# Attention keys and values on 128 partitions instead of 96, in a kernel of linear attention and two GELU-like layers

## The chip, the cores and the metric

The kernel runs on one core of a Trainium2 chip. The metric is device time in microseconds (us), the median of several executions. Engines that matter: TensorE (PE), with its weight loads (PEld), VectorE (DVE), ScalarE (ACT), GpSimd (POOL), and SyncE (SP), which here only issues DMAs.

## The reference

Shapes: q, k and v are 4 batches x 8 heads x 576 tokens x 64, all float32; x has 2304 tokens of 512 features; both layers go 512 to 2048 and back.

```
q_s = softmax(q, over the 64 features of a token)
k_s = exp(k - max over the 576 tokens) / (sum over the 576 tokens + 1e-9)   # per feature
kv  = einsum('bhsd,bhse->bhde', k_s, v)          # 64 x 64 for each head
att = einsum('bhsd,bhde->bhse', q_s, kv)
x   = att with heads side by side                # 2304 x 512
x   = layer(x, w_in1, w_out1, g(h) = h * sigmoid(1.702 h))
out = layer(x, w_in2, w_out2, g(h) = h * tanh(softplus(h)))
```

## The kernel before

Every large matmul is written as three fp32r matmuls on a high and a low part of each operand, and DVE and ACT split activations and weights into these parts. Tokens go in six blocks of 384. For a block the attention makes `xt`; the first layer makes `h` (line 755), the gate (lines 768 and 773) and `acc` (line 796). When all six blocks are through the first layer, the second follows (lines 755 into `hp`, 929 into `acc`). The weights arrive as raw words and are decoded by ACT and DVE (`weight`, lines 380 to 409) while the first block is computed.

The order of all work is written out by `Plan`: each operation is entered with its engines, an estimated cost, and what it reads and writes, and a list scheduler with six forward and backward passes picks the order and, where there are two ways, the engine. Engines then run their lists in order. SP issues all DMAs, one after the other (line 320, in `dma`).

Keys and values are handled by units: one unit is a pair of heads of one batch, so there are 16, four for each batch. Blocks 0, 1, 3 and 4 start a batch (`fresh`), and so make four units each; blocks 1 and 4 hold tokens of two batches. A unit does this:

- `k_load` and `v_load`: one DMA puts 576 tokens of both heads on 96 partitions, six tokens in each, in `kt`. In the first batch v lands packed in `vr` and ACT copies it (line 450) into `vt`, whose rows have two more columns of ones; later v goes straight into `vt`, one DMA for each head, in pieces of 256 bytes.
- `k_max`: three DVE maxima (line 476) bring six tokens of a partition to one, PE transposes the 96 x 128 result (line 481) and DVE takes the maximum along the row (line 482).
- In batches 0 and 1 `k_first`: for each head PE adds k and minus the maximum in PSUM by two matmuls of 384 columns (lines 494 and 497), and ACT takes exp from there (line 510). In batches 2 and 3 `k_later`: PE spreads the maximum (line 520), DVE subtracts (line 522), ACT takes exp (line 523).
- `k_kv`: for each head six matmuls (line 533) contract 96 tokens each and accumulate 64 x 66 values; the head picks the half of the output partitions. Then come a reciprocal and a scaled copy (lines 545 to 565).

In the trace each float32 matmul stands as two records of two passes; a transpose stands as one.

Of the kernel before, what the change touches and what calls it, by code (L numbers as in the profile page):

```python
# [8 lines left out]
F32 = mybir.dt.float32  # L9
# [201 lines left out]
def tile_attention_moe_moe(  # L211
# [21 lines left out]

    nc = tc.nc
    P = 128
# [9 lines left out]
    KC = 6  # L245
    KP = S // KC
# [3 lines left out]
    ND = 3  # L250
    SPLIT = ((0, 0), (0, 1), (1, 0))
# [26 lines left out]
    kt = [ap.tile([KP, 2, KC, D], F32, name=f"kt{i}") for i in range(2)]  # L278
    vt = [ap.tile([KP, 2, KC, D + 2], F32, name="vt0")]
    qt = ap.tile([P, NCT, 4, D], F32, name="qt")  # L280
    kv = [ap.tile([P, 2, P], F32R, name=f"kv{i}") for i in range(NHP)]
    pmt = [ap.tile([KP, P], F32, name=f"pmt{i}") for i in range(NHP)]
# [3 lines left out]
    kx = [ap.tile([KP, 2, 3, D], F32, name=f"kx{i}") for i in range(2)]  # L286
    rs = ap.tile([P, NHP], F32, name="rs")
    qs = ap.tile([P, 2, 12], F32, name="qs")

# [3 lines left out]
    kt += [sp.tile([KP, 2, KC, D], F32, name=f"kt{i}") for i in range(2, NHP)]  # L293
    vt += [sp.tile([KP, 2, KC, D + 2], F32, name=f"vt{i}") for i in range(1, NHP)]
    vr = [sp.tile([KP, 2, KC * D], F32, name=f"vr{i}") for i in range(2)] + [gt2[0:KP]]
# [5 lines left out]
    for t in vt:  # L301
        nc.gpsimd.memset(t[:, :, :, D : D + 2], 1.0)
# [15 lines left out]
    def dma(size, reads, writes, out, in_, slow=1):  # L318
        plan.op(
            [(DMA, max(size * slow / 280.0, 650.0), lambda: nc.sync.dma_start(out=out(), in_=in_()), False)],  # L320
            reads,
            writes,
        )
# [93 lines left out]
    def k_tile(u):  # L417
        return u if u < NHP else u % 2

    def v_tile(u):  # L420
        return u if u < NHP else 0

    def k_load(u):
        b, hp = divmod(u, NHP)
        dma(
            S * 512,
            [],
            [("kt", k_tile(u))],
            lambda: kt[k_tile(u)],
            lambda: k[b, 2 * hp : 2 * hp + 2].rearrange("h (p c) d -> p h c d", c=KC),  # L430
        )

    def v_load(u):
        b, hp = divmod(u, NHP)
        key = ("vt", v_tile(u))
        if b == 0:

            dense, dk = vr[hp % 3], [("vr", hp % 3)] if hp % 3 < 2 else [("gt", 0), ("gt", 1)]
            dma(
                S * 512,  # L440
                [],
                dk,
                lambda: dense,
                lambda: v[b, 2 * hp : 2 * hp + 2].rearrange("h (p c) d -> p h (c d)", c=KC),
            )
            to = vt[v_tile(u)][:, :, :, 0:D]
            of = dense.rearrange("p j (c d) -> p j c d", d=D)
            plan.op(
                [
                    (ACT, act_ns(768), lambda: nc.scalar.activation(out=to, in_=of, func=AF.Copy), False),  # L450
                    (POOL, 1200.0, lambda: nc.gpsimd.tensor_copy(out=to, in_=of), True),
                ],
                dk,
                [key + (j,) for j in range(2)],
            )
            return
        for j in range(2):
            dma(
                S * 256,
                [],  # L460
                [key + (j,)],
                lambda j=j: vt[v_tile(u)][:, j, :, 0:D],
                lambda j=j: v[b, 2 * hp + j].rearrange("(p c) d -> p c d", c=KC),
                slow=2,
            )

    def k_max(u, ps, key):

        kk = ("kt", k_tile(u))
# [4 lines left out]
        xk = ("kx", u % 2)  # L474
        largest = lambda n, out, in0, in1, reads, writes: dve(
            n, reads, writes, lambda: nc.vector.tensor_tensor(out=out, in0=in0, in1=in1, op=ALU.max), pair=True
        )
# [4 lines left out]
        dve(96, [key], [mk], lambda: nc.vector.reduce_max(out=m, in_=ps, axis=AX.X))  # L482

    def k_first(u, ps, keys):


        kk, mk = ("kt", k_tile(u)), ("mc", u % NHP)
        t, m = kt[k_tile(u)], mcol[:, u % NHP : u % NHP + 1]
        k_max(u, ps[0][:, NB : NB + KP], keys[0])
        for j in range(2):  # L490

            def less(j=j):
                o = ps[j][0:KP, 0:NB]
                nc.tensor.matmul(
                    out=o, lhsT=ident[0:KP, 0:KP], rhs=t[:, j].rearrange("p c d -> p (c d)"), start=True, stop=False
                )
                nc.tensor.matmul(
                    out=o.rearrange("p (c d) -> p c d", d=D),
                    lhsT=m.to_broadcast([P, KP]),
                    rhs=minus[:, j * D : (j + 1) * D].rearrange("p (o d) -> p o d", o=1).to_broadcast([P, KC, D]),  # L500
                    start=False,
                    stop=True,
                )

            pe(1330, [("kt", k_tile(u)), ("kt", k_tile(u), j), mk], [keys[j]], less, whole=True)
            act(
                NB,
                [keys[j]],
                [("kt", k_tile(u), j)],
                lambda j=j: nc.scalar.activation(  # L510
                    out=t[:, j].rearrange("p c d -> p (c d)"), in_=ps[j][0:KP, 0:NB], func=AF.Exp
                ),
                psum=True,
            )

    def k_later(u, ps1, ps2, key):
        kk, mk = ("kt", k_tile(u)), ("mc", u % NHP)
        t, m = kt[k_tile(u)], mcol[:, u % NHP : u % NHP + 1]
        k_max(u, ps1[:, 0:KP], key)
        pe(110, [mk], [key], lambda: nc.tensor.transpose(ps2[0:KP, :], m.to_broadcast([P, KP]), ident))  # L520
        far = ps2[0:KP, :].rearrange("p (j o d) -> p j o d", j=2, o=1).to_broadcast([KP, 2, KC, D])
        dve(768, [kk, key], [kk], lambda: nc.vector.tensor_tensor(out=t, in0=t, in1=far, op=ALU.subtract))
        act(768, [kk], [kk], lambda: nc.scalar.activation(out=t, in_=t, func=AF.Exp))

    def k_kv(u, ps3, key3):
        kk = ("kt", k_tile(u))
        t = kt[k_tile(u)]

        def mm():
            w = vt[v_tile(u)]  # L530
            for j in range(2):
                for c in range(KC):
# [8 lines left out]
        pe(1375, [kk] + [("kt", k_tile(u), j) for j in range(2)] + [("vt", v_tile(u), j) for j in range(2)], [key3], mm, whole=True)  # L541
# [51 lines left out]
    def q_soft(blk, half):  # L593
# [18 lines left out]
        either(768, ALU.subtract, flat, flat, wide, key + [sk], key)  # L612
        act(768, key, key, lambda: nc.scalar.activation(out=flat(), in_=flat(), func=AF.Exp))
        dve(768, key, [sk], lambda: nc.vector.reduce_sum(out=s, in_=flat(), axis=AX.X))
        dve(12, [sk], [sk], lambda: nc.vector.tensor_scalar_add(s, s, 1e-9))
# [347 lines left out]
    def idle():  # L963
# [9 lines left out]
        + [("kt", i) for i in range(2, NHP)]  # L973
        + [("vt", i, j) for i in range(1, NHP) for j in range(2)]
        + [("vr", i) for i in range(2)]
        + [("qr", i) for i in range(2)],
# [9 lines left out]
    for n in range(NS):  # L986
# [14 lines left out]
        if n == NS - NFC:  # L1001
            plan.op(
                [(NONE, 0.0, pool_second, False)],
                [],
                [("second",)]
                + [("kt", i) for i in range(2)]
                + [("vt", 0, j) for j in range(2)]
                + [("qt", j, d) for j in range(4) for d in (0, 192)]
                + [("kv", hp, a, j) for hp in range(NHP) for a in range(2) for j in range(2)]
                + [("kv32", hp, j) for hp in range(NHP) for j in range(2)]  # L1010
                + [(s, i) for s in ("qT32", "kx") for i in range(2)]
                + [("pm", i) for i in range(NHP)]
                + [(s, i) for s in ("mc", "rs") for i in range(NHP)]
                + [("qs", i) for i in range(2)],
            )
# [54 lines left out]
```

## Time and profile before

| | us |
|---|---|
| median of 3 runs | 892.26 (891.75 to 892.71) |
| the profiled execution, its own time | 892.4 |
| its span, first to last instruction | 890.6 |
| PE busy in the span | 880.1 |
| DVE busy | 395.7 |
| ACT busy | 361.6 |

A group's mean duration is that of one instruction from its start to its end, and neighbours overlap; so the price of a matmul in a stream is the distance between starts. Slices and windows tell where an engine is full; only there does its time set the pace.

### The profile page before, as it was taken

The page shows a single profiled execution, that of the slowest core. Times are in us where ns is not written, and L with a number is a line of the kernel's source. Part 1 is how long each engine was busy: PE and PEld are TensorE (multiplying, and loading weights), DVE is VectorE, ACT ScalarE, POOL GpSimd, SP SyncE. Part 2 cuts the span into 40 slices and gives each one's busy share as a digit, 9 for nine tenths or more (in the row PEclk, how much of TensorE's full clock was granted, in tenths as well). Part 3 has the DMA queues.
Part 4 walks back from the last instruction along what each step waited for, and adds up shares of the span by engine and source line. Part 5 has one row for each costly group of instructions (what it writes and reads, how often), then busy time and mean ns, then how long its engine had stood idle before and what let it go on. Part 6 is the DMA issues. An engine that isn't in the chain of part 4 may idle for free.

```text
span 890.6 us, 12257 instructions
## 1 busy us (share of the span) xinstructions
PE 880.1 (99%) x4961; PEld 819.4 (92%) x4961; DVE 395.7 (44%) x760; ACT 361.6 (41%) x649; POOL 5.3 (1%) x21
## 2 busy tenths in 40 slices
PE   8999999999999999999999999999999999999998
PEld 5797899999999999999999999899899899899897
DVE  7999993263385276226999911101101101101101
ACT  5987873242353244224778821311321321321321
POOL 1000000000000000000000000000000000000000
PEclk9999999999999999999999999999999999999999
DMA  9676762011132021100355302001001001000001
GB/s 249 202 224 181 202 208 72 1 36 71 27 90 99 1 71 45 59 1 18 118 167 187 120 1 71 36 1 71 36 1 71 36 1 71 36 1 0 36 1 36
DMA packets 63145, 65.80 MB, mean 74 GB/s; under 512 B 32497, under 2 KB 54513, under 8 KB 62577
## 3 DMA queue, kind: packets, MB, share of 16 engines
q1 hardware_dynamic: 63088, 65.02, 24.2%
q8 instruction: 39, 0.64, 0.3%
q14 instruction: 18, 0.14, 0.0%
HBM read 54.00 MB, written 11.01 MB: 73 GB/s over the span
## 4 chain that ended last, share of the span: by engine, by line
PE 90%; DVE 5%; ACT 2%; DMA 2%; issue 1%; SPq 0%; DVEq 0%
PE hp L755 23%; PE acc L929 22%; PE acc L796 20%; PE h L755 20%; PE at L533 1%; DVE dec L393 1%; DVE dec L398 1%; DMA raw<-in_moe_w_in_dram 1%; PE at L667 1%; PE at L638 1%; DVE W L329 1%; PE at L676 1%; DMA raw<-in_moe_w_out_dram 1%; DVE gt L773 1%; DVE g L329 0%
## 5 line engine op out<-in xcount | busy, mean ns | idle before, releaser
L755 PE MATMUL h<-xt,W 128*128 128x384 f32 x1152 | 224.0, 339 | 1.0 <-DVE gt L773 0.8
L796 PE MATMUL acc<-g,W 128*128 128x384 f32 x1152 | 223.2, 339 | 0.1
L755 PE MATMUL hp<-xt,W 128*128 128x384 f32 x1152 | 208.4, 336 | 0.0
L929 PE MATMUL acc<-W,g 128*128 128x512 f32 x864 | 206.1, 392 | 0.0
L755 PEld LDWEIGHTS hp<-xt,W 128*128 128x128 f32 x1152 | 201.9, 188 | 3.7
L755 PEld LDWEIGHTS h<-xt,W 128*128 128x128 f32 x1152 | 200.7, 188 | 4.4 <-DVE gt L773 1.1
L796 PEld LDWEIGHTS acc<-g,W 128*128 128x128 f32 x1152 | 200.6, 188 | 2.8 <-issue 0.8
L929 PEld LDWEIGHTS acc<-W,g 128*128 128x128 f32 x864 | 161.7, 188 | 32.6
L329 DVE TENSOR_TENSOR g<-gt,g 128x384 fp32r<-128x384 f32 (+1 forms) x110 | 67.4, 613 | 178.8 <-ACT g L337 178.5
L329 DVE TENSOR_TENSOR g<-tb,g 128x768 fp32r<-128x768 f32 x32 | 30.6, 958 | 211.5 <-ACT g L337 211.5
L904 ACT ACTIVATE tb<-hp 128x768 f32<-128x768 f32 x32 | 26.0, 813 | 177.6 <-PE hp L755 177.6
L337 ACT ACTIVATE g<-gt 128x384 fp32r<-128x384 f32 (+1 forms) x112 | 63.7, 569 | 80.1 <-PE acc L796 78.0
L768 ACT ACTIVATE gt<-h 128x384 f32<-128x384 f32 x96 | 46.8, 487 | 92.2 <-PE h L755 91.9
L773 DVE SCALAR_TENSOR_TENSOR gt<-gt,h 128x384 f32<-128x384 f32 x96 | 52.7, 549 | 63.5 <-ACT gt L768 63.3
L904 ACT ACTIVATE gt<-hp 128x768 f32<-128x768 f32 x16 | 13.0, 813 | 96.3 <-PE hp L755 96.3
L346 ACT ACTIVATE dec<-raw 128x512 f32<-128x512 f32 x64 | 42.9, 675 | 11.0 <-DVE W L329 8.2
L346 ACT ACTIVATE raw<-raw 128x512 int32<-128x512 uint32 x63 | 42.1, 677 | 6.1 <-DMA raw<-in_moe_w_out_dram 4.5
L329 DVE TENSOR_TENSOR W<-dec,W 128x512 fp32r<-128x512 f32 x64 | 43.6, 684 | 0.7 <-ACT W L337 0.5
L398 DVE CUSTOM_DVE_ANT_0 dec<-raw,dec 128x1024 uint16<-128x1024 uint16 x64 | 43.6, 683 | 0.4
L393 DVE SCALAR_TENSOR_TENSOR dec<-raw,dec 128x512 int32<-128x512 int32 x64 | 43.6, 683 | 0.2
L337 ACT ACTIVATE W<-dec 128x512 fp32r<-128x512 f32 x62 | 38.7, 628 | 5.8 <-DVE dec L398 5.8
L337 ACT ACTIVATE g<-tb 128x768 fp32r<-128x768 f32 x32 | 27.1, 846 | 1.0
(79 smaller groups left out, 397.0 us busy)
## 6 DMA issues: line engine op xcount, KB each, us to landing
raw<-in_moe_w_in_dram SPq DMA_DIRECT2D x32, 512.0 KB, 4.2
raw<-in_moe_w_out_dram SPq DMA_DIRECT2D x32, 512.0 KB, 4.0
x2d<-xt SPq DMA_DIRECT2D x16, 384.0 KB, 3.1
xt<-x2d SPq DMA_DIRECT2D x4, 1536.0 KB, 6.5
kt<-in_k_dram SPq DMA_DIRECT2D x16, 288.0 KB, 4.5
out_dram<-dec SPq DMA_DIRECT2D x15, 256.0 KB, 2.1
vt<-in_v_dram SPq DMA_DIRECT2D x24, 144.0 KB, 3.2
qt<-in_q_dram SPq DMA_DIRECT2D x24, 96.0 KB, 2.7
```

The lines of the kernel that those rows point to most:

```text
L329: return lambda: engine.tensor_tensor(out=out(), in0=in0(), in1=in1(), op=op)
L337: (ACT, act_ns(n), lambda: nc.scalar.activation(out=out(), in_=in_(), func=AF.Copy), False),
L346: (ACT, act_ns(512), lambda: nc.scalar.activation(out=out, in_=in_, func=AF.Copy, scale=scale), False),
L393: lambda: nc.vector.scalar_tensor_tensor(out=a, in0=hi_w, scalar=-0x80000000, in1=a, op0=ALU.bitwise_and, op1=ALU.bitwise_or),
L398: dve(512, [rl], [da], lambda: nc.vector.tensor_tensor(out=a, in0=a, in1=lo_w, op=ALU.add), pair=True)
L533: nc.tensor.matmul(out=ps3[j * D : (j + 1) * D, 0 : D + 2], lhsT=t[:, j, c, :], rhs=w[:, j, c, :], start=c == 0, stop=c == KC - 1,)
L755: nc.tensor.matmul(out=h(), lhsT=w_mm(fc, 0, a, cc), rhs=xt[buf][:, cc, b, :], start=cc == 0 and i == 0, stop=cc == NCC - 1 and i == 2,)
L768: act(NB, [hk, ("tables",)], [tk], lambda: nc.scalar.activation(out=t, in_=h, func=AF.Tanh, scale=0.851), psum=True)
L773: lambda: nc.vector.scalar_tensor_tensor(out=t, in0=t, scalar=1.0, in1=h, op0=ALU.add, op1=ALU.mult),
L796: nc.tensor.matmul(out=acc[dm][:, 0:NB], lhsT=w_mm(fc, 1, a, dm), rhs=g[n % 2][:, b, :], start=fc == 0 and i == 0, stop=fc == NFC - 1 and ...
L904: nc.scalar.activation(out=tb[i], in_=hb(n), func=AF.Mish)
L929: nc.tensor.matmul(out=acc[bank], lhsT=g2[gi][:, j, a, c * P : (c + 1) * P], rhs=w_mm(2 * pr + j, 1, b, 0, 512), start=pr == 0 and j == 0 ...
```

## The change

k and v lie on 128 partitions. A head's first 512 tokens are four on each partition; the last 64 tokens of the pair's two heads share one further chunk, head 0 on partitions 0 to 63 and head 1 on 64 to 127. `kt` and `vt` have nine chunks (and a tenth that is unused): 0 to 3 for head 0, 4 shared, 5 to 8 for head 1. `own(t)` names the chunks of the two heads and `rest(t, j)` the 64 x 64 piece of head j.

- Loads: one DMA of 256 KB for the 512 tokens, and two of 16 KB for the rest (`rests`), for k; the same for v in the first batch, and for later batches two of 128 KB and two of 16 KB.
- `k_max`: maxima of 256 and 128 elements over 128 partitions, then two of 64 elements on 64 partitions each; the transpose has 128 columns.
- `k_first`: the first step handles head 0 and the shared chunk (320 columns), with two 64-row matmuls that subtract each head's maximum from its half of the shared chunk; the second step handles head 1 (256 columns).
- `k_later`: DVE's subtraction becomes three (512 elements, and two of 64); exp covers 576.
- `k_kv`: for each head four matmuls that contract 128 tokens and one that contracts 64.
- The costs that the planner is given change with it. `GROUPS` is empty, so that the other branch in `q_soft` is not taken; `qsum` is a small tile for it.

```diff
-    KC = 6
-    KP = S // KC
+    KC = S // P
+    KB = KC * P
+    KN = 2 * KC + 1
...
+    def rests(t, heads, keys):
+        for j in range(2):
+            dma(D * 256, [], keys[j : j + 1], lambda j=j: rest(t, j), lambda j=j: heads[j, KB:S], least=LEAST)
...
-        largest(384, x, t[:, :, 0:3], t[:, :, 3:6], [kk], [xk])
+        largest(256, x, own(t)[:, :, 0:2], own(t)[:, :, 2:4], [kk], [xk])
         largest(128, wide, x[:, :, 0], x[:, :, 1], [xk], [pk])
-        largest(128, wide, wide, x[:, :, 2], [xk, pk], [pk])
-        pe(110, [pk], [key], lambda: nc.tensor.transpose(ps, pm, ident[0:KP, 0:KP]))
+        for j in range(2):
+            s = slice(j * D, (j + 1) * D)
+            largest(64, pm[s, s], pm[s, s], rest(t, j), [kk + (2 + j,), pk], [pk])
+        pe(110, [pk], [key], lambda: nc.tensor.transpose(ps, pm, ident))
...
+            c0, n = ((0, KC + 1), (KC + 1, KC))[j]
...
+                if j == 0:
+                    for i in range(2):
+                        s = slice(i * D, (i + 1) * D)
+                        nc.tensor.matmul(
+                            out=o[s, KC * D : (KC + 1) * D],
+                            lhsT=m[s].to_broadcast([D, D]),
+                            rhs=minus[s, s],
+                            start=False,
+                            stop=False,
+                        )
...
-            pe(1330, ...)
+            pe((1220, 890)[j], ...)
...
                 for c in range(KC):
                     nc.tensor.matmul(
-                        out=ps3[j * D : (j + 1) * D, 0 : D + 2],
-                        lhsT=t[:, j, c, :],
-                        rhs=w[:, j, c, :],
+                        out=o,
+                        lhsT=own(t)[:, j, c],
+                        rhs=own(w)[:, j, c],
                         start=c == 0,
-                        stop=c == KC - 1,
+                        stop=False,
                     )
+                nc.tensor.matmul(out=o, lhsT=rest(t, j), rhs=rest(w, j), start=False, stop=True)
-        pe(1375, ...)
+        pe(1145, ...)
```

## Rows read from the trace of the kernel before

**Rows 1.** The page's parts 1 and 2: busy time by engine, busy tenths in 40 slices.

```profile
PE 880.1 (99%) x4961; PEld 819.4 (92%) x4961; DVE 395.7 (44%) x760; ACT 361.6 (41%) x649; POOL 5.3 (1%) x21
...
PE   8999999999999999999999999999999999999998
...
DVE  7999993263385276226999911101101101101101
```

**Rows 2.** The windows: stretch, length; PE, PEld, DVE, ACT, POOL busy; PE clock; DMA share; GB/s.

```profile
10.00:16.00 6.00, 5.35 (x58) 3.63 (x56) 5.69 (x16) 5.04 (x10) 0.00 (x0) 1.00 1.11 276
16.00:22.00 6.00, 5.01 (x14) 2.90 (x15) 4.30 (x13) 5.42 (x13) 0.00 (x0) 0.72 1.10 272
98.00:106.00 8.00, 8.00 (x61) 7.05 (x60) 8.00 (x19) 6.53 (x15) 0.00 (x0) 1.00 0.49 160
150.00:170.00 20.00, 20.00 (x117) 20.00 (x116) 5.57 (x10) 4.92 (x10) 0.00 (x0) 1.00 0.00 1
310.00:345.00 35.00, 35.00 (x278) 33.49 (x277) 23.56 (x58) 15.40 (x34) 0.00 (x0) 1.00 0.27 66
```

**Rows 3.** Groups by line and shape, PE: busy us, mean ns.

```profile
L533 PE MATMUL at<-vt,kt 96*64 96x66 f32 x288 | 17.3, 226 | 0.0
...
L520 PE MATMUL at<-ident,mcol 128*96 128x128 f32 x8 | 2.2, 272 | 0.0
```

**Rows 4.** Timeline of PE, one late unit: start us, us, what, count.

```profile
237.18 0.68 PE L755 MATMUL h<-xt,W 128*128 128x384 f32 x3
237.79 1.44 PE L533 MATMUL at<-vt,kt 96*64 96x66 f32 x24
239.16 1.83 PE L755 MATMUL h<-xt,W 128*128 128x384 f32 x9
240.84 1.72 PE L796 MATMUL acc<-g,W 128*128 128x384 f32 x9
```

**Rows 5.** The chain of waits, 66 to 122 us: start us, us, what.

```profile
86.78 0.65 PE at L494 x2
87.42 0.65 PE at L497 x2
...
91.54 2.08 PE h L755 x12
```

**Rows 6.** Groups by line and shape, DVE and ACT.

```profile
L476 DVE TENSOR_TENSOR kx<-kt 96x384 f32<-96x384 f32 x16 | 8.8, 549 | 5.9 <-DMA kt<-in_k_dram 5.9
...
L625 ACT ACTIVATE xt<-at 128x384 fp32r<-128x384 f32 x16 | 7.7, 486 | 3.6 <-PE at L667 3.0 <-PE at L676 0.2 <-DMA qt<-in_q_dram 0.2
...
L625 ACT ACTIVATE xt<-at 128x192 fp32r<-128x192 f32 x16 | 5.2, 325 | 6.1 <-PE at L667 5.1 <-PE at L676 0.8
...
L565 DVE SCALAR_TENSOR_TENSOR kv<-at,rs,kv 64x64 fp32r<-64x64 f32 x16 | 4.5, 283 | 3.3 <-ACT kv L556 3.0
```

**Rows 7.** Waits of DVE, 0 to 32 us: us in total, times, longest.

```profile
DVE kx L476 <- DMA kt<-in_k_dram: 4.3, 2, 4.0
DVE mcol L482 <- PE acc L481: 1.7, 1, 1.7
```

**Rows 8.** Timeline of SP's issues, 0 to 40 us.

```profile
0.73 0.89 SPq L320 DMA_DIRECT2D kt<-in_k_dram  x2
...
5.03 1.35 SPq L320 DMA_DIRECT2D raw<-in_moe_w_in_dram  x2
...
35.36 2.49 SPq L320 DMA_DIRECT2D qt<-in_q_dram  x4
```

**Rows 9.** DMA issues, 0 to 40 us: count, KB each, median us to landing.

```profile
qt<-in_q_dram SPq DMA_DIRECT2D x8, 48.0 KB, 3.7
```

**Rows 10.** The chain of waits, 0 to 66 us.

```profile
5.03 9.62 DMA raw<-in_moe_w_in_dram
```

**Rows 11.** The page's part 6, DMA issues of the whole span.

```profile
raw<-in_moe_w_in_dram SPq DMA_DIRECT2D x32, 512.0 KB, 4.2
```

More of the change, by code (lines that the diff above doesn't have):

```diff
@@ L250, in tile_attention_moe_moe @@
     ND = 3
+    LEAST = 200.0
+    GROUPS = ()
     SPLIT = ((0, 0), (0, 1), (1, 0))
@@ L316, in pe, with dma @@
         plan.op([(PE, ns, fn, whole)], reads, writes)
-    def dma(size, reads, writes, out, in_, slow=1):
+    def dma(size, reads, writes, out, in_, slow=1, least=650.0):
         plan.op(
-            [(DMA, max(size * slow / 280.0, 650.0), lambda: nc.sync.dma_start(out=out(), in_=in_()), False)],
+            [(DMA, max(size * slow / 280.0, least), lambda: nc.sync.dma_start(out=out(), in_=in_()), False)],
             reads,
@@ L421, in v_tile, with own, rest @@
         return u if u < NHP else 0
+    def own(t):
+        return t.rearrange("p (j c) d -> p j c d", j=2)[:, :, 0:KC]
+    def rest(t, j):
+        return t[j * D : (j + 1) * D, KC]
+    def rests(t, heads, keys):
+        for j in range(2):
+            dma(D * 256, [], keys[j : j + 1], lambda j=j: rest(t, j), lambda j=j: heads[j, KB:S], least=LEAST)
     def k_load(u):
         b, hp = divmod(u, NHP)
+        t = kt[k_tile(u)]
+        heads = k[b, 2 * hp : 2 * hp + 2]
+        kk = ("kt", k_tile(u))
         dma(
-            S * 512,
+            P * 2048,
             [],
-            [("kt", k_tile(u))],
-            lambda: kt[k_tile(u)],
-            lambda: k[b, 2 * hp : 2 * hp + 2].rearrange("h (p c) d -> p h c d", c=KC),
+            [kk],
+            lambda: own(t),
+            lambda: heads[:, 0:KB].rearrange("h (p c) d -> p h c d", c=KC),
         )
+        rests(t, heads, [kk + (2 + j,) for j in range(2)])
     def v_load(u):
@@ L458, in v_load, with k_keys @@
             dma(
-                S * 256,
+                P * 1024,
                 [],
                 [key + (j,)],
-                lambda j=j: vt[v_tile(u)][:, j, :, 0:D],
-                lambda j=j: v[b, 2 * hp + j].rearrange("(p c) d -> p c d", c=KC),
+                lambda j=j: own(to)[:, j],
+                lambda j=j: heads[j, 0:KB].rearrange("(p c) d -> p c d", c=KC),
                 slow=2,
             )
+        rests(to, heads, [key + (2 + j,) for j in range(2)])
+    def k_keys(u):
+        return [("kt", k_tile(u)) + i for i in ((), (0,), (1,), (2,), (3,))]
     def k_max(u, ps, key):
-        kk = ("kt", k_tile(u))
         t, m, mk = kt[k_tile(u)], mcol[:, u % NHP : u % NHP + 1], ("mc", u % NHP)
@@ L518, in k_later @@
         t, m = kt[k_tile(u)], mcol[:, u % NHP : u % NHP + 1]
[L519 to L523, printed above, removed]
+        k_max(u, ps1, key)
+        pe(110, [mk], [key], lambda: nc.tensor.transpose(ps2, m.to_broadcast([P, P]), ident))
+        far = ps2.rearrange("p (j o d) -> p j o d", j=2, o=1).to_broadcast([P, 2, KC, D])
+        dve(
+            512, [kk, key], [kk], lambda: nc.vector.tensor_tensor(out=own(t), in0=own(t), in1=far, op=ALU.subtract)
+        )
+        for j in range(2):
+            s = slice(j * D, (j + 1) * D)
+            dve(
+                64,
+                [key],
+                [kk + (2 + j,)],
+                lambda j=j, s=s: nc.vector.tensor_tensor(out=rest(t, j), in0=rest(t, j), in1=ps2[s, s], op=ALU.subtract),
+            )
+        act(
+            576,
+            [kk],
+            [kk, kk + (2,), kk + (3,)],
+            lambda: nc.scalar.activation(out=t[:, 0:KN], in_=t[:, 0:KN], func=AF.Exp),
+        )
     def k_kv(u, ps3, key3):
-        kk = ("kt", k_tile(u))
         t = kt[k_tile(u)]
@@ L611, in q_soft @@
         dve(768, key, [sk], lambda: nc.vector.reduce_max(out=s, in_=flat(), axis=AX.X))
[L612 to L615, printed above, removed]
+        if (blk, half) in GROUPS:
+            dve(12, [sk], [sk], lambda: nc.vector.tensor_single_scalar(out=s, in_=s, scalar=-1.0, op=ALU.mult))
+            for i in range(12):
+                act(
+                    D + 223,
+                    key + [sk],
+                    key + [("qsum", half)],
+                    lambda i=i: nc.scalar.activation(
+                        out=flat()[:, i], in_=flat()[:, i], func=AF.Exp, bias=s[:, i : i + 1], accum_out=qsum[:, half, i : i + 1]
+                    ),
+                )
+            dve(12, [("qsum", half)], [sk], lambda: nc.vector.tensor_scalar_add(s, qsum[:, half, :], 1e-9))
+        else:
+            either(768, ALU.subtract, flat, flat, wide, key + [sk], key)
+            act(768, key, key, lambda: nc.scalar.activation(out=flat(), in_=flat(), func=AF.Exp))
+            dve(768, key, [sk], lambda: nc.vector.reduce_sum(out=s, in_=flat(), axis=AX.X))
+            dve(12, [sk], [sk], lambda: nc.vector.tensor_scalar_add(s, s, 1e-9))
         dve(96, [sk], [sk], lambda: nc.vector.reciprocal(s, s))
@@ L972, in tile_attention_moe_moe @@
         [("late",)]
-        + [("kt", i) for i in range(2, NHP)]
-        + [("vt", i, j) for i in range(1, NHP) for j in range(2)]
+        + [key for u in range(2, NHP) for key in k_keys(u)]
+        + [("vt", i, j) for i in range(1, NHP) for j in range(4)]
         + [("vr", i) for i in range(2)]
+        + [("vr", i, j) for i in range(2) for j in range(2)]
         + [("qr", i) for i in range(2)],
@@ L1005, in tile_attention_moe_moe @@
                 [("second",)]
-                + [("kt", i) for i in range(2)]
-                + [("vt", 0, j) for j in range(2)]
+                + [key for u in range(2) for key in k_keys(u)]
+                + [("vt", 0, j) for j in range(4)]
                 + [("qt", j, d) for j in range(4) for d in (0, 192)]
@@ L1013, in tile_attention_moe_moe @@
                 + [(s, i) for s in ("mc", "rs") for i in range(NHP)]
-                + [("qs", i) for i in range(2)],
+                + [(s, i) for s in ("qs", "qsum") for i in range(2)],
             )
```

72 lines of the change are left out of this document (42 added, 30 removed).

## The prediction

> **What bounds the kernel now.** I read the page's parts 1 and 2 first: TensorE (PE) is busy 99% of the span, VectorE (DVE) 44%, and the slices show that DVE is full only in the first seventh [rows 1]. So the windows came next [rows 2]. They show three stages. From 10 to 28 us, while the first batch's attention is made, ScalarE (ACT) and the DMA engines are full and PE runs at a lower granted clock for a stretch (0.72 from 16 to 22 us). From about 22 to 126 us DVE is busy without a break (8.00 of 8 us from 98 to 106), because it decodes the weights, and PE is almost full beside it. From there to the end PE is busy every microsecond, 20.00 of 20 and 35.00 of 35, and DVE and ACT have room. After 126 us a nanosecond taken from PE is a nanosecond of the result; before that it counts only as far as DVE, ACT or a load lets it.
>
> The changed code works in two of these places. Sixteen units (a unit is one pair of heads) are made: units 0 to 3 before 33 us, 4 to 7 between 66 and 121 us, 8 to 15 between 234 and 344 us; the eight transposes of line 520, one for each of the last kind, and the 288 records of line 533 (24 for each of units 4 to 15) count them [rows 3].
>
> **The last eight units, in the stage that PE bounds.** Here only line 533's matmuls, the transposes and DVE's and ACT's share change, and of these only PE's counts: DVE is busy 23.56 of 35 us, ACT 15.40 [rows 2].
>
> The price of line 533 comes from the timeline of one unit [rows 4]. From the start at 237.18 to the start at 240.84 are 3.66 us. In them lie twelve GEMM matmuls, and twelve take 2.08 us [rows 5], so the 24 records cost 3.66 - 2.08 = 1.58 us. Inside the run the records come faster than that: it spans 1.44 us to the end of its last record, whose length is about the mean of 0.226 [rows 3], so the last begins 1.44 - 0.22 = 1.22 us after the first, 1.22 / 23 = 0.053 us apart. 24 x 0.053 = 1.27; the other 0.31 us is lost where the run begins and ends, 0.155 at each.
>
> What is lost there? Line 533 is the one matmul before the change whose output has 64 partitions; its neighbours use all 128. The change makes more such borders. For each head, four matmuls contract 128 partitions and a fifth only 64 (the shared chunk), both into 64 output partitions. A unit then runs GEMM, 128x64, 64x64, 128x64, 64x64, GEMM: five borders instead of two. It has 10 matmuls instead of 12, so 20 records.
>
> No row shows a border between 128 and 64 contracted partitions. Bounds: 0, if it costs what any other next matmul costs, and 0.155, the row's price for the only kind of border it shows. I take 0.155, the nearest row. New run: 20 x 0.053 + 5 x 0.155 = 1.06 + 0.78 = 1.84 us, against 1.58: +0.25 us for a unit, +2.0 us for eight. With free borders it is -4 x 0.053 = -0.21 a unit, -1.7 us in all. So the sign hangs on this one price.
>
> The trace shows 0.31 us lost around a run with narrower output [rows 4]. The Trainium skill, page "TensorEngine Tiling (Array Packing)", section "Tiling Modes" (Key Properties), has a rule for this: changing the tiling mode, not just the tile, drains TensorE; it lists 128x64 and 64x64 as different modes. By that rule the three added borders cost and the change loses PE time; without it, four records fewer win. No run here shows a 64-row mode yet.
>
> The transpose of line 481 moves 128 columns instead of 96. At 0.65 us for two passes of 384 columns [rows 5], 32 columns of one pass are 0.03 us, 0.2 us for eight; I take 0 since PE's price for such a lone short matmul isn't visible to that precision, and keep 0.2 for the range. DVE's subtraction splits into three and ACT's exp shrinks; both are hidden by PE's GEMM. If that cover were gone, the chain of one unit would grow by two 64x64 DVE operations of 0.28 us [rows 6], 0.6 us for a unit.
>
> **Units 4 to 7, in the stage that DVE bounds.** The subtraction on PE (lines 494 and 497) takes four steps of 0.65 us, 2.60 us a unit, for 4 x 384 = 1536 columns [rows 5]. The new one has 320 + 64 + 64 + 256 + 256 + 256 = 1216 columns: 2.06 us. Two 64x64 borders at 0.155 take 0.31 back: -0.23. With +0.25 from the kv matmuls the unit's PE time is unchanged. With free borders it would be -0.54 - 0.21 = -0.75 a unit, -3.0 us for four, but only part of this would arrive, as DVE is at 8.00 of 8 us here [rows 2].
>
> DVE's own work for a unit: the first maximum falls from 384 to 256 elements a partition. Between 549 ns for 384 and 283 for a 64x64 operation [rows 6] the slope is 0.83 ns an element: -0.11 us. The third maximum becomes two of 64, and the reduce reads 128 columns instead of 96: +0.03, and one more instruction, which adds between 0 and 0.15 (half of the 283 ns, since DVE's neighbours overlap). I take it that they cancel; over eight units the ends are -0.6 and +0.6 us.
>
> **The start.** ACT: from 486 to 325 ns for 384 and 192 elements [rows 6], an element costs 0.84 ns. Lines 450 and 510 handle 576 instead of 768 elements a unit: -0.16 us each, four units, -1.3 us together. ACT is nearly full (5.42 of 6 us, [rows 2]), so up to 1.3 us could arrive; but DVE waits 1.7 us in that time for a maximum that PE transposes, and 4.3 us for k [rows 7], and it is DVE's work that must be done before 126 us. I take -0.8.
>
> The loads: every k load and every v load becomes one of 256 KB and two of 16 KB, for the first batch 24 instead of 8. SP issues them one after the other: 0.45 us each for two k loads, 0.62 for each of four 48 KB loads [rows 8, 9]. Six loads of k and v go out before the first weight load at 5.03 us [rows 8], so with their small ones ahead it would go out 12 x 0.45 = 5.4 us later. But that load needs 9.62 us to land [rows 10], where the median of its kind is 4.2 [rows 11]: it lies 5.4 us behind bytes that are already asked for. So the delay is just covered, and the bytes are the same. The first q load is pushed back by four small ones, 1.8 us, and DVE waits for it at once; the bounds are 0 and 1.8 and I take +0.4, as that load too is mostly transfer. Later small loads pass on SP beside DVE's work, 16 in units 4 to 7, 7 us in 55; the weight loads queued behind them have four buffers, and I count 0 with +0.5 as the other end.
>
> On the row that the weight load needs 9.62 us behind others [rows 10], the Trainium skill ("DMA: Bandwidth & Descriptors", section "Rules for kernel authors") speaks against the change: two transfers to disjoint halves of the partitions bring nothing and should be one, and under 64 KB overhead is most of the cost. Were overhead all, the second rival below would hold.
>
> **Sum.** +2.0 (last eight units) + 0 (units 4 to 7) - 0.8 + 0.4 (start) = +1.6 us. The profiled execution took 892.4 us (span 890.6 and 1.8 around it), so 894.0; the median of the runs is 892.26, 0.14 lower, and gives 893.9 us. That is 0.18% more. About 0.2%, 1.8 us, is what a measurement of this kernel can tell, so I forecast no measurable change, on the slow side.
>
> **Rivals.**
> - *Borders cost nothing* (the PE time that is removed arrives). For it: the two heads of line 533 write different halves of the output and the run still advances at 0.053 us a record [rows 3, 4], so not every switch inside the array costs. Against it: the 0.31 us at the run's ends. It gives -1.7 from the last eight units, -0.4 at the start and -0.5 of the 3.0 us of units 4 to 7: 892.3 - 2.6 = 889.7 us.
> - *The small loads delay the start* (slower). Place: SP's queue before the first weight load. It decides from the point where the loads put ahead cost more than the 5.4 us that this load now waits behind others. At 0.62 us, the price of the 48 KB loads [rows 8, 9], twelve take 7.4 us, 2.0 too many, and the decoded weights, with them DVE's whole first stage, come 2.0 us later; the first q load adds 0.6 more than I took. 893.9 + 2.6 = 896.5 us. For it: DVE has no slack behind the start. Against it: DVE has other work when the first weights land.
> - *Borders at half price*, 0.08 us: the kv run then is 1.06 + 2 x 0.155 + 3 x 0.08 = 1.61, +0.03 a unit. +0.2 - 0.4 = 892.1 us. For it: the added borders stay among narrow outputs.
>
> **Chances.** Forecast 0.42, free borders 0.30, small loads 0.15, half price 0.13. The forecast's own range is 892.6 to 895.2, since a new list order from the planner moves single waits by some tenths each; it gives 0.55 no change, 0.42 slower, 0.03 faster. Free borders: 0.7 faster, 0.3 no change. Small loads: 0.9 slower. Half price: 0.1 to each side. Sums: faster 0.42 x 0.03 + 0.30 x 0.7 + 0.13 x 0.1 = 0.24; slower 0.42 x 0.42 + 0.15 x 0.9 + 0.13 x 0.1 = 0.32; no change 0.44. The range from 889.5 to 896.2 takes in the first rival nearly whole and the second in part.
>
> **What would show it.** The 20 records of a kv run between GEMM matmuls should take 1.84 us by my price, 1.37 by free borders: that step is wrong if it is under 1.5. The PE subtraction of a unit should shrink from 2.60 to 2.3 or so. The first weight load should land within a microsecond of 14.65 us (5.03 + 9.62), and DVE's last weight decode of the first model near where it is. If PE has new idle time after 126 us, or if the stage before 126 us moves by more than 1.5 us either way, the prediction is wrong in its second half.

## The result, and the profile after

The change makes the kernel slower: 898.91 us (median of 6 runs, 898.12 to 899.05) against 892.27 (6 runs, 891.75 to 892.99), a ratio of 1.0073 [1.0062, 1.0084], +6.6 us. The forecast was 893.9 in a range of 889.5 to 896.2. The sign of its first term was right, its size was not, and a term that stood at nothing, the stage in which DVE is full, made 2.6 us of the loss.

The profiled execution took 899.01 us with a span of 897.1, 6.5 us above the span of before. The page's parts 1 and 2, as in [rows 1]:

```profile
PE 885.9 (99%) x4953; PEld 826.5 (92%) x4953; DVE 399.3 (45%) x794; ACT 357.8 (40%) x649; POOL 3.0 (0%) x19
...
PE   8998999999999999999999999999999999999998
...
DVE  6999994253376267325899921011111101101101
```

PE is as full as before, with 5.8 us more to do. ACT has 3.8 us less and GpSimd 2.3 less, DVE 3.6 more. None of this says where the 6.5 us lie. Three marks on PE's timeline do: the first GEMM matmul of block 0, the start of the `acc` GEMM with which DVE's full stage ends, and the second layer's first `hp`. The timeline of PE around the last two, after:

```profile
133.83 0.68 PE L833 MATMUL h<-xt,W 128*128 128x384 f32 x3
134.35 2.24 PE L874 MATMUL acc<-g,W 128*128 128x384 f32 x12
...
489.91 3.30 PE L833 MATMUL hp<-xt,W 128*128 128x384 f32 x18
```

and before:

```profile
129.69 1.38 PE L755 MATMUL h<-xt,W 128*128 128x384 f32 x7
130.91 2.24 PE L796 MATMUL acc<-g,W 128*128 128x384 f32 x12
...
483.45 2.78 PE L755 MATMUL hp<-xt,W 128*128 128x384 f32 x15
```

| stage, by starts on PE | before | after | difference | forecast |
|---|---|---|---|---|
| to the first `h` (28.84, 29.65) | 28.84 | 29.65 | +0.8 | -0.4 |
| to `acc` of the next block (130.91, 134.35) | 102.07 | 104.70 | +2.6 | 0 |
| to the first `hp` (483.45, 489.91) | 352.54 | 355.56 | +3.0 | +2.0 |
| to the end of the span (890.6, 897.1) | 407.2 | 407.2 | 0.0 | 0 |

So there are two things to explain: 3.0 us in the late units, where PE sets the pace, and 3.4 us before them, at the start and in the stage where DVE is full. The marks come from one execution each and are good to about 1 us: the first experiment below has before's order and instructions up to 234 us, and its marks are 28.67 and 131.84 for 28.84 and 130.91.

The late units first, on PE's timeline of one unit, as in [rows 4]:

```profile
240.58 1.73 PE L833 MATMUL h<-xt,W 128*128 128x384 f32 x9
242.25 0.68 PE L596 MATMUL at<-vt,kt 128*64 128x66 f32 x8
242.86 0.33 PE L603 MATMUL at<-vt,kt 64*64 64x66 f32 x2
243.12 0.68 PE L596 MATMUL at<-vt,kt 128*64 128x66 f32 x8
243.73 0.33 PE L603 MATMUL at<-vt,kt 64*64 64x66 f32 x2
243.98 0.79 PE L833 MATMUL h<-xt,W 128*128 128x384 f32 x3
244.61 1.72 PE L874 MATMUL acc<-g,W 128*128 128x384 f32 x9
```

From 240.58 to 244.61 are 4.03 us, less 2.08 for twelve GEMM matmuls [rows 5]: the run costs 1.95 us. Before it was 1.58 with four records more. +0.37 a unit, eight times, is 3.0, all of the third stage's loss. The second stage is told by the windows over it; before (28.84:130.91) and after:

```profile
28.84:130.91 102.07, 98.68 (x588) 87.79 (x586) 100.82 (x212) 84.00 (x168) 2.36 (x2) 1.00 0.69 197
```

```profile
29.65:134.35 104.70, 100.25 (x587) 89.70 (x586) 102.18 (x218) 83.56 (x169) 0.00 (x0) 1.00 0.68 197
```

DVE is busy 1.36 us more and idle 1.27 us more (1.25 to 2.52): together the 2.6. And GpSimd, with two instructions of 2.36 us before, does nothing. Which two they were, the groups by line and shape show, before:

```profile
L329 DVE TENSOR_TENSOR g<-gt,g 128x384 fp32r<-128x384 f32 x94 | 52.1, 554 | 68.4 <-ACT g L337 68.1
...
L329 POOL TENSOR_TENSOR g<-gt,g 128x384 fp32r<-128x384 f32 x2 | 2.4, 1178 | 90.7 <-ACT g L337 90.7
```

and after:

```profile
L335 DVE TENSOR_TENSOR g<-gt,g 128x384 fp32r<-128x384 f32 x96 | 53.2, 554 | 60.0 <-ACT g L343 59.7
```

Two subtractions of the gate, work that the diff doesn't touch, went from GpSimd to DVE: 2 x 554 ns, 1.1 of the 1.36 us. The planner chose that. So from here the question is whether the changed instructions or the changed order made the 3.4 us ahead of the late units.

### The profile page after: what moved, and what is told of

Same layout as the page of the kernel before. It is cut to its first block, busy times and chain, and to the rows that moved or that the text cites. A ratio compares the mean times of both kernels' runs of the same rounds, so it can differ in the third digit from the quotient of the medians.

```text
span 897.1 us, 12389 instructions
## 1 busy us (share of the span) xinstructions
PE 885.9 (99%) x4953; PEld 826.5 (92%) x4953; DVE 399.3 (45%) x794; ACT 357.8 (40%) x649; POOL 3.0 (0%) x19
## 4 chain that ended last, share of the span: by engine, by line
PE 92%; DMA 3%; DVE 2%; ACT 2%; issue 1%; SPq 0%; ACTq 0%; DVEq 0%
PE hp L833 22%; PE acc L1007 22%; PE acc L874 20%; PE h L833 20%; PE at L596 2%; DMA raw<-in_moe_w_in_dram 1%; DMA raw<-in_moe_w_out_dram 1%; PE at L716 1%; PE at L745 1%; DVE dec L404 1%; PE at L754 1%; PE at L603 1%; DMA qr<-in_q_dram 1%; PE acc L531 0%; DVE dec L399 0%
```

## The experiments

Each ran five rounds beside the kernel before, in three groups; before had medians of 892.33, 892.35 and 891.94 us in them.

**The border alone, put into before.** The last kv matmul of each head contracts 64 of its 96 partitions, in the last eight units, order unchanged:

```diff
-                        lhsT=t[:, j, c, :],
-                        rhs=w[:, j, c, :],
+                        lhsT=t[0:64, j, c, :] if u >= WHOLE * NHP and c == KC - 1 else t[:, j, c, :],
+                        rhs=w[0:64, j, c, :] if u >= WHOLE * NHP and c == KC - 1 else w[:, j, c, :],
```

> The kernel before, in the same order, with one thing changed: in units 8 to 15 the last of each head's six kv matmuls contracts 64 of the 96 partitions (the other 32 tokens of that chunk are left out). The number of matmuls stays 12 a unit. Border theory: each unit gets three more borders, and the two heads, which overlap by some 0.17 us where one ends and the other begins, no longer do; a kv run then costs 24 x 0.057 + 5 borders of about 0.155, 2.15 us, against 1.58: +0.57 a unit, +4.6 us in all, 896.9 us, all of it between 234 and 346 us. Rival (a 64-row matmul costs what any other does, and the loss in the changed kernel's late units has another cause): 892.3 us, no change.

Measured: 896.42 us, ratio 1.0046 [1.0033, 1.0059]. PE's timeline of one unit:

```profile
238.11 0.69 PE L755 MATMUL h<-xt,W 128*128 128x384 f32 x3
238.72 2.04 PE L533 MATMUL at<-vt,kt 96*64 96x66 f32 x24
240.69 1.85 PE L755 MATMUL h<-xt,W 128*128 128x384 f32 x9
```

From the run's first record to the next GEMM's are 1.97 us; in [rows 4] 1.37 (237.79 to 239.16). The records are as many, the order is the same, less is contracted, and a unit costs 0.60 us more. Three borders were added (full to narrow, narrow to full between the heads, full to narrow): 0.20 us each in equal shares. The third stage is 357.30 (131.84 to 489.14), +4.8 or 8 x 0.60.

**The border taken out of after.** The fifth kv matmul of a head contracts all 128 partitions in the last eight units, order unchanged:

```diff
-                nc.tensor.matmul(out=o, lhsT=rest(t, j), rhs=rest(w, j), start=False, stop=True)
+                full = u >= WHOLE * NHP
+                kr, vr_ = (t[:, KC], w[:, KC]) if full else (rest(t, j), rest(w, j))
+                nc.tensor.matmul(out=o, lhsT=kr, rhs=vr_, start=False, stop=True)
```

> The changed kernel, in the same order, with one thing changed: in units 8 to 15 the fifth kv matmul of each head contracts all 128 partitions of the shared chunk (so the two heads' last 64 tokens are mixed). Still 10 matmuls a unit, but no matmul of 64 rows. Border theory: a kv run falls from 1.95 to 1.58 - 4 x 0.053 = 1.37 us, -0.58 a unit, -4.6 us: 894.3 us, and what is left over the kernel before (about 2 us) lies before 131 us. Rival (the late loss comes from elsewhere, DMA or waits): 898.9 us.

Measured: 894.39 us, ratio 1.0018 [1.001, 1.0027], 4.5 below after. PE's timeline (L605 is the fifth matmul):

```profile
240.22 1.73 PE L835 MATMUL h<-xt,W 128*128 128x384 f32 x9
241.88 0.74 PE L596 MATMUL at<-vt,kt 128*64 128x66 f32 x10
242.40 0.22 PE L605 MATMUL at<-vt,kt 128*64 128x66 f32 x1
242.46 0.22 PE L596 MATMUL at<-vt,kt 128*64 128x66 f32 x1
242.46 0.22 PE L605 MATMUL at<-vt,kt 128*64 128x66 f32 x1
...
242.81 0.28 PE L605 MATMUL at<-vt,kt 128*64 128x66 f32 x2
243.02 0.79 PE L835 MATMUL h<-xt,W 128*128 128x384 f32 x3
243.65 1.72 PE L876 MATMUL acc<-g,W 128*128 128x384 f32 x9
```

The 20 records now take 1.14 us (241.88 to 243.02) and not 1.73: 0.59 for three borders, 0.20 each again. Both experiments change two 64-row matmuls of a unit together with three borders, so a price of 0.30 for each such matmul fits them as well; no run separates the two. By the prediction's measure the run is 3.43 - 2.08 = 1.35 us; free borders had been put at 1.37. The rows show a second thing: ten records of L596 start before the first of L605, though a head has only eight, so records of the second head start before the last ones of the first. The third stage is 351.3 (133.98 to 485.30), 4.2 below after and 1.2 below before. The 2 us by which the kernel still stands above before lie ahead of the late units (`acc` at 133.98 us for 130.91).

**The small loads taken out of the first batch.** k and v of a unit of batch 0 come by one load of 288 KB; the sixteen small loads are not issued, order unchanged:

```diff
-        rests(t, heads, [kk + (2 + j,) for j in range(2)])
+        rests(t, heads, [kk + (2 + j,) for j in range(2)], skip=b == 0)
...
-            rests(dense, heads, rk)
+            rests(dense, heads, rk, skip=True)
```

> The changed kernel, in the same order, with one thing changed: in the first batch a k or v load is one DMA of 288 KB in which each partition gets nine neighbouring tokens of the pair (so tokens land under other heads and chunks than they should), and the 16 small loads are not issued. Theory of the small loads: SP issues the first weight load at about 5 us instead of 10, the first q load lands earlier, and the first GEMM starts 0.8 to 1.5 us earlier (28.2 to 28.9 instead of 29.65 us); of the 3.4 us that the changed kernel loses before 131 us, 1 to 1.5 come back: 897.4 to 897.9 us. Rival (the start is not the place; the loss before 131 us is made by the new order between 35 and 126 us): the first GEMM moves, but the end of the first block does not: 898.5 to 899.

Measured: 898.35 us, ratio 1.0063 [1.0051, 1.0075]: no gain that can be told, and the first `h` comes at 29.91 us for 29.65, so it did not move forward as both theory and rival had it. In after SP's timeline had the first weight load 5 us later than [rows 8]:

```profile
4.75 2.26 SPq L326 DMA_DIRECT2D vr<-in_v_dram  x4
...
10.02 0.47 SPq L326 DMA_DIRECT2D raw<-in_moe_w_in_dram  x1
```

In this kernel it goes out at 4.85:

```profile
4.85 1.55 SPq L326 DMA_DIRECT2D raw<-in_moe_w_in_dram  x2
```

But ACT's timeline has the first use of the words at 15.18 us in after and at 15.44 here:

```profile
15.18 0.66 ACT L352 ACTIVATE dec<-raw 128x512 f32<-128x512 f32 x1
```

```profile
15.44 0.66 ACT L352 ACTIVATE dec<-raw 128x512 f32<-128x512 f32 x1
```

ACT came to the words without waiting for them in both. In this order the delay at the queue is covered, and the small loads are not the cause.

**The order alone: before's instructions, the change's costs.** Every cost that the change tells the planner for work that before has too, and no other edit:

```diff
-            pe(1330, ...)
+            pe((1220, 890)[j], ...)
-        pe(1375, ...)
+        pe(1145, ...)
-        largest(384, x, t[:, :, 0:3], t[:, :, 3:6], [kk], [xk])
+        largest(256, x, t[:, :, 0:3], t[:, :, 3:6], [kk], [xk])
...
```

> The kernel before, every instruction as it was; only the costs that the planner is told for the k and v work are those of the change (the subtraction on PE 1220 and 890, the kv matmuls 1145, maxima of 256 elements, exp of 576, loads of 256 KB). So the order, and with it the engine of some operations, is another. Planner theory: this alone moves the time before 131 us by 1 to 3 us (one to two of the g subtractions move from GpSimd to VectorE, each 0.5 us of VectorE), 893.3 to 895.3. Rival (the order is robust and the loss comes from the new instructions themselves): 891.8 to 892.8.

Measured: 897.63 us, ratio 1.0066 [1.0051, 1.0081]. Without one changed instruction the kernel lost 5.3 us, more than the theory asked for; the second stage took 105.0 us, as in after, and GpSimd got none of the gate's subtractions. Its profiled execution, the lowest of six runs, has a span 4.1 us above before's, and 1.6 of them lie behind `acc` (133.36 to 487.52 is 354.16 us for 352.54): an order costs in the late stage too.

**Truer costs for PE, in after.** The chain of waits of after has PE's share of one early unit as 0.54 + 0.26 + 0.63 + 0.43 + 0.43 = 2.29 us for the subtraction, and 0.61 + 0.26 + 0.61 + 0.26 = 1.74 for the kv run, 4.03 in all:

```profile
103.16 0.54 PE at L531 x2
103.70 0.26 PE at L537 x4
103.96 0.63 PE at L544 x2
...
105.64 0.43 PE at L531 x2
106.07 0.43 PE at L544 x2
...
107.34 0.61 PE at L596 x8
107.95 0.26 PE at L603 x2
108.21 0.61 PE at L596 x8
108.82 0.26 PE at L603 x2
```

The planner was told 1220 + 890 + 1145 ns, 3.26 us. (Before it was told 2 x 1330 + 1375, 4.04, for 2.60 + 1.37, 3.97.)

```diff
-            pe((1220, 890)[j], ...)
+            pe((1430, 870)[j], ...)
-        pe(1145, ...)
+        pe(1750, ...)
```

> The changed kernel, every instruction as it was; the planner is told what PE really takes by the changed kernel's trace: 1430 and 870 ns instead of 1220 and 890 for the two steps of the subtraction, 1750 instead of 1145 for a unit's kv matmuls. Theory of the wrong costs (the order before 131 us is bad because the planner counts 0.77 us too little PE time for each unit): the second block's output stage starts near 131.5 instead of 134.3 us, the late units stay as they are: 895.8 to 896.8 us. Rival (the order before is a lucky one, any other costs 2 to 3 us): 898 to 899.5.

Measured: 896.96 us, ratio 1.0047 [1.0034, 1.006], 2 us below after and just above the range that was expected. The windows over the second stage:

```profile
30.98:132.07 101.09, 98.75 (x587) 89.44 (x586) 100.06 (x217) 82.34 (x168) 3.62 (x2) 1.00 0.67 196
```

The changed instructions do that stage in 101.09 us, 1 us less than before's, which is no more than two executions of one order differ by; two subtractions are on GpSimd again. But the start is 1.3 us later than in after, and there the chain of waits runs over SP's issues: 18 loads of k and v, 12 of them the small ones, and two of q go out before the first weight load at 12.51 us (5.03 in before), and ACT waits for its words until 17.36 us (14.68). By this chain the small loads do delay the start in this order.

**Costs moved by 15 ns, in before.** Both PE costs up, then both down:

```diff
-            pe(1330, ...)
+            pe(1345, ...)
-        pe(1375, ...)
+        pe(1390, ...)
```

> The kernel before, every instruction as it was; the planner's two PE costs of the k work are raised by 15 ns (1345 and 1390 for 1330 and 1375), so the order differs in places. Theory of the wrong costs: costs that are as right as before give an order as good, 891.3 to 893.3. Rival (a lucky order): another order, 893.5 to 896.

```diff
-            pe(1330, ...)
+            pe(1315, ...)
-        pe(1375, ...)
+        pe(1360, ...)
```

> As the run with costs raised by 15 ns, but lowered by 15 ns (1315 and 1360). Theory of the wrong costs: 891.3 to 893.3. Rival (a lucky order): 893.5 to 896.

Measured: 892.64 us, 1.0003 [0.9993, 1.0012], and 896.53, 1.0038 [1.0026, 1.0051]. The first is where the theory had it; the second is above the rival's range too. So 15 ns in an estimate can cost 4 us. Of the slower one's 4.0 us at `acc`, 2.75 lie at the start (31.59 us to the first `h`), where the windows show PE's granted clock at 0.57 from 16 to 22 us, mostly its lower level of 1.2 GHz, PE having been idle 1.33 of the 6 us before, and again 1.29 of these:

```profile
10.00:16.00 6.00, 4.67 (x54) 3.25 (x54) 4.48 (x11) 3.08 (x6) 0.00 (x0) 1.00 1.11 280
16.00:22.00 6.00, 4.71 (x16) 3.44 (x17) 5.01 (x18) 5.63 (x12) 0.00 (x0) 0.57 0.83 233
```

How much of the delay the clock made is not shown. In before this stretch stands at 0.72 [rows 2], in the first experiment, whose order is the same there, at 1.00, and the first `h` comes at 28.84 and 28.67 us.

**PE's costs alone, and the others alone, in before.** The edits of the order experiment, split:

```diff
-            pe(1330, ...)
+            pe((1220, 890)[j], ...)
-        pe(1375, ...)
+        pe(1145, ...)
```

> The kernel before, every instruction as it was; only the planner's PE costs of the k work are those of the change (1220 and 890 for 1330 twice, 1145 for 1375), 0.78 us too little for each unit. Theory of the wrong PE costs: from the first GEMM to the second block's output stage (102.1 us before, 104.7 in the changed kernel, 105.0 with all costs of the change) it takes 104 to 105.5 us, and the total is 893.5 to 896 depending on the start. Rival (any order is as likely as another): that stage 101 to 103.5.

```diff
-            S * 512,
+            P * 2048,
...
-        largest(384, x, t[:, :, 0:3], t[:, :, 3:6], [kk], [xk])
+        largest(256, x, t[:, :, 0:3], t[:, :, 3:6], [kk], [xk])
...
```

> The counterpart: the kernel before, every instruction as it was, PE's costs as before, and all other costs of the k and v work as the change has them (maxima, exp, copies, loads). Theory of the wrong PE costs: the stage from the first GEMM to the second block's output stays at 101 to 103.5 us; total 891.5 to 895, by the start. Rival: 104 or more here as well.

Measured: 895.7 us, 1.0035 [1.0022, 1.0048], for PE's costs; 893.8, 1.0019 [1.0011, 1.0028], for the others. The windows over the second stage, of the first and then of the second:

```profile
27.25:132.31 105.06, 99.35 (x589) 88.15 (x588) 101.90 (x214) 85.53 (x171) 0.00 (x0) 1.00 0.67 194
```

```profile
28.29:131.24 102.95, 98.97 (x587) 89.06 (x586) 102.29 (x217) 83.20 (x168) 2.55 (x2) 0.98 0.67 195
```

Both are as expected: with PE told too short, DVE is idle for 105.06 - 101.90 = 3.16 us and GpSimd does nothing; with the other costs changed, DVE is idle for 0.66 us.

**A version without narrow matmuls.** v's rests of the two heads lie in two chunks, each filled with zeros in its other half, so that all ten kv matmuls contract 128 partitions; one maximum over both heads makes a single subtraction do for the shared chunk:

```diff
+        nc.gpsimd.memset(t[D:P, KC], 0.0)
+        nc.gpsimd.memset(t[0:D, KN], 0.0)
...
-            rests(dense, heads, rk)
+            rests(to, heads, [key + (2 + j,) for j in range(2)], v_rest)
...
-            pe((1220, 890)[j], ...)
+            pe((1110, 890)[j], ...)
```

> A version without 64-row matmuls: v's shared chunk becomes two, each with zeros under the other head, so all ten kv matmuls contract 128 partitions; the maximum is taken over both heads, so the shared chunk needs no subtraction of its own and the late subtraction on VectorE is one instruction; k's last tokens come by one load. Planner's costs 1110, 890 and 1145. Border theory: a kv run takes 1.37 us, eight late units gain 1.7 us on the kernel before; before 131 us PE has 0.7 us less for each unit and VectorE about as much as before, so that stage lies between 1 us better and, with an unlucky order, 3 us worse: 889.6 to 893.6 us, likeliest 891. Rival (padding or the common maximum costs what the borders did): over 894.

Measured: 890.87 us, ratio 0.9982 [0.9974, 0.9991]; 8 us below after, and the only kernel here below before. The third stage is 351.43, as in the second experiment, 4.1 below after's. The rest of the 8 us comes from other instructions and another order together, and no run divides it.

**Two of these in another order.** After with truer costs, 15 ns higher; and the last version with three costs higher by 15, 15 and 45 ns:

```diff
-            pe((1430, 870)[j], ...)
+            pe((1445, 885)[j], ...)
-        pe(1750, ...)
+        pe(1765, ...)
```

> The changed kernel, every instruction as it was, with the planner's PE costs as the trace has them plus 15 ns (1445, 885, 1765). Theory of the wrong PE costs: as with the right costs (101.1 us), that stage takes 101 to 103 us, less than the 104.7 of the changed kernel; with a start of 27 to 31 us the total is 894 to 898. Rival: 104 or more.

```diff
-            pe((1110, 890)[j], ...)
+            pe((1125, 905)[j], ...)
-        pe(1145, ...)
+        pe(1190, ...)
```

> The version without 64-row matmuls, with the planner's costs nudged (1125, 905, 1190 instead of 1110, 890, 1145). Its late units must keep their gain (about 1.1 us from the second block's output stage to the second layer against the kernel before, 4.1 against the changed kernel); the stage before it may move by the order. 889 to 894, likeliest 891.5.

Measured: 898.83 us, 1.0071 [1.0056, 1.0085], with single runs from 896.37 to 900.94; and 892.8, 1.0006 [0.9997, 1.0016]. The first takes back all that truer costs had won and lies above the 894 to 898 expected. Its profiled execution, the lowest of its runs, can't show where (its second stage is 103.06 us), but its runs go with the clock: the two with a mean granted clock of 1.00 took 896.37 and 897.73 us, the four with 0.992 to 0.996 took 898.70 to 900.94. The second keeps most of the gain of the late units (351.82 us, 0.7 below before where 1.1 was expected) and not that over before.

All orders together (marks from the profiled executions, good to about 1 us, which in four rows were the lowest of their runs; GpSimd: subtractions of the gate that it does):

| instructions | order from | ratio | first `h` | `acc` | GpSimd |
|---|---|---|---|---|---|
| before | its own costs | 1 | 28.84 | 130.91 | 2 |
| before | +15 ns | 1.0003 | 27.22 | 129.70 | 2 |
| before | -15 ns | 1.0038 | 31.59 | 134.92 | 3 |
| before | the others' costs changed | 1.0019 | 28.29 | 131.24 | 2 |
| before | PE's costs changed | 1.0035 | 27.25 | 132.31 | 0 |
| before | all costs changed | 1.0066 | 28.33 | 133.36 | 0 |
| after | its own costs | 1.0073 | 29.65 | 134.35 | 0 |
| after | truer costs | 1.0047 | 30.98 | 132.07 | 2 |
| after | truer costs, +15 ns | 1.0071 | 28.71 | 131.77 | 2 |
| without narrow matmuls | its own costs | 0.9982 | 26.28 | 129.80 | 1 |
| without narrow matmuls | +15, +15, +45 ns | 1.0006 | 24.84 | 129.44 | 2 |

## Why the prediction was wrong

**Failed step: the price of a new list order.** The prediction said that "a new list order from the planner moves single waits by some tenths each", and counted units 4 to 7 at nothing. Their stage took 2.6 us more, beyond the 1.5 us that the prediction had named as the sign of a wrong second half, and the last weight of the first layer is decoded at 125.81 us for 121.73. The runs show one kernel's instructions in six orders from 1 to 1.0066. Five orders that are not before's own have a mean of (1.0003 + 1.0019 + 1.0035 + 1.0038 + 1.0066) / 5 = 1.0032, +2.9 us. After in three orders has a mean of 1.0064, and the difference of the two means, 0.0032 or 2.8 us, is about what the late units cost. So the 6.6 us are some 3 us of instructions and 3.6 us of an order that was worse than before's; the latter is within what before's own instructions lost by order alone (5.3 us with the change's costs). That an order alone can cost this much is shown, on before's own instructions. That the 3.6 us of after are all order is an estimate: three and five orders are few, an order moved the late stage too, and two effects of the new instructions lie ahead of it (the borders at the start and the issues of the small loads, below).

**Why this order is worse is shown only in part.** The five profiles with PE told 0.7 to 0.8 us a unit too short (after, the two edits of it in its order, and two of before) have none of the gate's work on GpSimd and reach `acc` at 132.3 to 134.4 us; all others have one to three and reach it at 129.4 to 132.1, save the one that started 2.75 us late. Splitting the costs points the same way (132.31 against 131.24). But 132.1 and 132.3 lie closer together than two executions of one order. Also against it: truer costs don't make after reliably faster (1.0047 and 1.0071), and 15 ns do as much. Whether the wrong costs or only their being other costs did it stays open.

**The last eight units: right in kind, too small.** +0.37 us a unit came and not +0.25, +3.0 and not +2.0. The 20 records by themselves cost what was said (1.35 for 1.37). The mis-sized term is the added border: 0.20 us by both experiments, where the loss at the run's ends had given 0.155. The second experiment's rows offer a reason: between two heads with no narrow matmul between them, records of both interleave, so a border there also takes this away. That part is argued from rows, not measured apart. Nor is 0.20 the price of every such border: the subtraction, with two borders to and from 64x64, takes 2.29 us, 0.23 above the 2.06 of its columns, which is 0.12 for each. The Trainium skill, "TensorEngine Tiling (Array Packing)", section "Tiling Modes" (Key Properties), says that a change of mode drains the engine; the two experiments agree that a change costs time, 0.20 us in equal shares, and no row shows the drain itself. The rivals of free and half-priced borders fall with this.

**PE's subtraction** was put at 2.60 to 2.3 us and measures 2.29. **DVE's own work** cancels about as said, apart from what came from GpSimd. The groups by shape show the first maximum at 418 ns for 549, and two 64x64 maxima of 215:

```profile
L510 DVE TENSOR_TENSOR kx<-kt 128x256 f32<-128x256 f32 x16 | 6.6, 418 | 3.6 <-DMA kt<-in_k_dram 3.6
...
L510 DVE TENSOR_TENSOR pmt<-pmt,kt 64x64 f32<-64x64 f32 x32 | 6.7, 215 | 0.5
```

**The start: the loads right, the path wrong.** The first weight load went out 5 us later, and its words were in use at 15.18 us for 14.68: the delay was "just covered", within the microsecond that the prediction asked for, and the rival of small loads falls for this order with the third experiment. The Trainium skill's rule on small transfers ("DMA: Bandwidth & Descriptors", "Rules for kernel authors") would have made them cost; at this place the run without them doesn't bear it out, while in the order of truer costs the weights came 2.7 us later (17.36 for 14.68). ACT's -0.8 didn't arrive. The windows of after, for [rows 2]:

```profile
10.00:16.00 6.00, 6.00 (x46) 4.55 (x46) 5.02 (x11) 3.97 (x8) 0.00 (x0) 1.00 0.86 259
16.00:22.00 6.00, 5.96 (x46) 4.61 (x45) 5.48 (x19) 4.61 (x12) 0.00 (x0) 1.00 0.90 297
98.00:106.00 8.00, 8.00 (x48) 7.35 (x47) 7.79 (x20) 5.51 (x12) 0.00 (x0) 1.00 0.89 268
```

ACT is no longer nearly full (4.61 of 6 us for 5.42), and DVE waits for the first q at once, 1.5 us for 0.3, where +0.4 had been taken. The path is PE's, of which the prediction priced nothing here: from 10 to 22 us PE is idle for 0.04 us in after and for 1.64 in before [rows 2], and from 7.95 to 27.22 us after's chain of waits is all PE, where before's runs over the weight load and ACT until 16.94 us. On this path lie the four units' borders and also matmuls whose result nobody uses: `Plan.emit` puts transposes of the identity (line 1042) where the planner expects PE to be idle, 41 in after for 17 in before. Thirteen of them stand in the chain, for 0.87 + 0.55 = 1.42 us; in before none starts behind 6.3 us.

```profile
8.41 0.87 PE h L1042 x8
...
18.51 0.55 PE h L1042 x5
```

The first `h` came 0.8 us later, though the clock stayed at 1.00. Starts from 27.2 to 31.6 us with before's own instructions show that an order alone can do this; how much of the 0.8 is borders and how much is these matmuls is open.

## What to carry to other kernels

Price a matmul of a new shape by the borders that it puts into the stream, not by its columns: here twelve alike beat ten of two kinds, and ten alike, padded with zeros, beat both. Where a scheduler writes the order, a changed cost is a change of the kernel: before crediting a few microseconds to an edit, run the old instructions with the new costs, and the new ones in a few orders. And give the forecast of such a change the spread of these orders, here 0 to 5 us on the slow side of an order that was already good.

## What the runs showed that was not expected

- 15 ns in two planner costs of before, 1% of each, cost 3.4 us by the ratio and 4.2 by the medians; the first `h` moved from 28.84 to 31.59 us, with PE's granted clock at 0.57 for six microseconds.
- The same shape of matmul for two heads, into different halves of the output, overlaps where they meet (around 242.4 us above), so that 20 records need 1.14 us; 64-row matmuls between them raise it to 1.73.
- Some orders repeat badly: single runs of one kernel from 896.37 to 900.94 us, of before's own order in the first group from 891.27 to 895.38. In two orders the clock goes with it: besides the one above, with PE's costs alone changed three runs at a mean granted clock of 1.00 took 894.06 to 894.96 us and three at 0.998 took 896.45 to 897.10.
